# Two more tiles' first layer half by seven products, odd values copied by transfers, and one sum of each weight kept in place

## The chip, the cores and the metric

The kernel runs on one core of one Trainium2 chip. The metric is the device time of one execution in microseconds (us); it is the median of several runs. Engines are named as the profile names them: PE (matrix products), PEld (the loading of their stationary operand), DVE (vector), ACT (scalar functions), POOL, and SP, which here only issues transfers. A small q behind a name is that engine's sequencer.

## The reference

Sliding-window attention over 8 batches of 8 heads with 576 positions of 64 values each, followed by two matrix products with a gated function between them. All rows of the attention output go through the two layers.

```python
scores = scale * np.matmul(q, k.transpose(0, 1, 3, 2))
mask = np.abs(pos[:, None] - pos[None, :]) <= 32
attn = softmax(np.where(mask, scores, -1e9))
x = np.matmul(attn, v)                     # -> 4608 rows of 512
h = x @ w_in                               # 512 x 2048
g = h * (1.0 / (1.0 + np.exp(-1.702 * h)))
out = g @ w_out                            # 2048 x 512
```

## The kernel before

The 4608 rows are 36 units of 128; two units make a tile `t` of 256 rows (18 tiles). The program first works through a head (tiles 0 to 2), then `window(4)`, then one `steady(w)` for each w from 5 to 18, and `close()`. In `steady(w)` PE makes the attention of units 2w and 2w+1, the first layer of tile w-1 and the second layer of tile w-2. Every engine executes its instructions in the order in which the program emits them.

A first layer can be made in two ways. `layer1(t, d)` is the plain one: eight products of 128x128 by 128x256 into one bank, then one ACT pass; eight such calls make a tile. The other way makes half of the tile's first layer (the columns 512 to 1023 and 1536 to 2047 of `w_in`) by the seven products of a fast 2x2 block multiplication, and the other half by four calls of `layer1`. `seven(t, n)` is one of these products: eight matrix instructions of 128x128 by 128x128. It needs sums of blocks of `w_in` (`wi_sum`, made once) and sums of blocks of the tile (`x_sums`, made by DVE). Partial results are moved out of the two banks `h_main` and `h_side` by `move`.

```python
def bank(self, kind, shape, dtype, name):        # PSUM: 8 banks in all, with the pair "a" below
    bufs = {"h": 2, "o": 1, "t": 1, "b": 2}[kind]
    return self.ps.tile(shape, dtype, name=name, tag=kind, bufs=bufs)

def pair(self, name, which=None):                # two banks: "a", or both buffers of "b"; in turn
    if which is None:
        which, self.turn = self.turn, 1 - self.turn
    if which == 0:
        return self.ps.tile([128, 2, 512], F32, name=name, tag="a", bufs=1)
    return [self.bank("b", [128, 512], F32, f"{name}{i}") for i in range(2)]

def odd_v(self, m, eng):                         # values shifted by 64 rows
    ...
    self.cast(eng, vo[64:128], self.ve[m % NV][64:128])
    self.cast(eng, vo[0:64], nxt)

def layer1(self, t, d, kind="h"):
    ...
    ffs = (d, d + 8) if t > 2 else (2 * d, 2 * d + 1)
    ...    # 2 x 4 products into one bank of the given kind, then ACT: g <- gelu(bank)

def norm(self, u):                               # DVE: x <- values / sum, frees the banks of values(u)
    ...

# head(), from the first layer of tile 2 on (cut)
    self.layer1(2, 0)
    self.values(6)
    self.norm(6)
    for n in range(2):
        self.w_sums(n, 1)
    for d in range(1, 3):
        self.layer1(2, d)
    self.x_T(6, "b")
    self.layer1(2, 3)
    for hp in range(4):
        self.rows_T("k", 2, hp, "t", dve)
        if hp in (1, 2):
            self.w_sums(hp + 1, 1)
        self.rows_T("q", 2, hp, "o", act)
        self.layer1(2, 4 + hp)
    for m in (7, 8, 9):
        self.odd_v(m, dve)

# window(4): its end (cut)
    self.loads(w)
    for m in (10, 11):
        self.odd_v(m, dve)
    self.w_in_sums((0, 1))
    for d in range(8):
        self.layer1(w - 1, d)
    self.g_sums(w - 1, 0)
    self.feed(w)
    self.w_in_sums((2, 3))

def steady(self, w):                             # cut to its order; t = w - 1, o = w - 2
    self.loads(w)
    self.scores(a, which=0); self.scores(b, which=1)
    self.g_sums(o, 1, (0, 1))
    self.product(o, 1, "o")
    self.keep(o, 1, dve)                         # reads the bank that product 6 adds to
    if w > 5:
        self.g_sums(o, 0, (2,))
    self.product(o, 2, "t")
    self.result(o, 11)
    ...
    self.product(o, 6)
    ...
    self.seven(t, 1); self.move("side", "main", dve); self.x_sums(t, (0, 1))
    self.values(a, which=0); self.values(b, which=1)
    self.norm(a); self.x_T(a)                    # x_T: a transposing transfer issued by SP
    ...
    self.norm(b); self.x_T(b)
    ...
    self.product(o, 4); self.result(o, 21, act)  # result 21 stores unit b of tile o (SP)
    ...
    self.feed(w)                                 # odd_v of units 2w+2, 2w+3; then rows_X (SP)
    ...
    self.product(o, 3); self.result(o, 12)       # stores unit a of tile o (SP)
```

`values(u)` of the next window reads what `odd_v(u)` made in this one. `rows_X` are four transposing transfers of later keys and queries.

Of the kernel before, what the change touches and what calls it, by code (L numbers as in the profile page):

```python
# [15 lines left out]
F32 = mybir.dt.float32  # L16
# [11 lines left out]
class _Kernel:  # L28
# [7 lines left out]
    def __init__(self, ctx, tc, q, k, v, w_in, w_out, out):  # L36
        self.tc, self.nc = tc, tc.nc
        self.q, self.k, self.v, self.w_in, self.w_out, self.out = q, k, v, w_in, w_out, out
        self.B, self.H, self.S, self.D = q.shape
        self.N = self.B * self.S  # L40
        self.DM = self.H * self.D
        self.DFF = w_in.shape[1]
        self.NK = self.DM // 128
        self.NFF = self.DFF // 128
        self.scale = 1.0 / (self.D ** 0.5)
        self.NU = self.N // 128
        self.NW = self.NU // 2

        def pool(name, bufs, **kw):
            return ctx.enter_context(tc.tile_pool(name=name, bufs=bufs, **kw))  # L50

        self.cst = pool("cst", 1)
        self.work = pool("work", 2)
        self.ps = pool("ps", 1, space=bass.MemoryType.PSUM)
        self.stage, self.paired = {}, set()
        self.span = {"A": (0, 320)}
        self.xT, self.g, self.o_ps = {}, {}, {}
        self.p, self.acc, self.x, self.sc = {}, {}, {}, {}
        self.gs, self.part, self.o_sb = {}, {}, {}
        self.xs, self.hs, self.turn = {}, {}, 0  # L60

    def bank(self, kind, shape, dtype, name):
# [15 lines left out]
    def setup(self):  # L78
# [3 lines left out]
        self.w_in_sb = cst.tile([128, self.NK, self.DFF], F16, name="w_in_sb")  # L82
        self.wi_sum = cst.tile([128, 4, 2, self.DFF // 4], F16, name="wi_sum")
        self.ident16 = cst.tile([128, 128], F16, name="ident16")
        self.w_out_sb = cst.tile([128, self.NFF, self.DM], F16, name="w_out_sb")
        self.w_sum = cst.tile([128, 4, self.NFF // 2, self.DM // 2], F16, name="w_sum")
        self.kT = cst.tile([128, 4, RING + 64], BF16, name="kT")
# [88 lines left out]
    def odd_v(self, m, eng):  # L176

        vo = self.vo[m % NV]
        nxt = self.v_first if m == self.NU - 1 else self.ve[(m + 1) % NV][0:64]
        self.cast(eng, vo[64:128], self.ve[m % NV][64:128])  # L180
        self.cast(eng, vo[0:64], nxt)

# [180 lines left out]
    def layer1(self, t, d, kind="h"):  # L363
# [5 lines left out]
        else:  # L369
            hps = self.bank(kind, [128, 2, 256], F32, "h_ps")  # L370
        ffs = (d, d + 8) if t > 2 else (2 * d, 2 * d + 1)
        for i in range(2):
# [21 lines left out]
    def w_sums(self, i, half):  # L394

        b, w, dve = self.w_out_sb, self.w_sum, self.nc.vector
        top, low = slice(4 * half, 4 * half + 4), slice(8 + 4 * half, 12 + 4 * half)
        left, right = slice(0, 256), slice(256, 512)
        t = [w[:, n, top, :] for n in range(4)]
        a, c = [(b[:, top, right], b[:, top, left]), (b[:, low, right], t[0]),  # L400
                (b[:, low, right], b[:, top, right]), (b[:, low, left], t[1])][i]
        dve.tensor_sub(t[i], a, c)
# [19 lines left out]
    def product(self, t, n, kind=None):  # L422
# [10 lines left out]
        for k in range(8):  # L433
            x, y = {1: (g[:, k, u], b[:, k, left]), 2: (g[:, 8 + k, u], b[:, 8 + k, left]),
                    3: (gs[:, 3, k], b[:, 8 + k, right]), 4: (g[:, 8 + k, v], w[:, 3, k]),
                    5: (gs[:, 0, k], w[:, 0, k]), 6: (gs[:, 1, k], w[:, 1, k]), 7: (gs[:, 2, k], w[:, 2, k])}[n]
            nc.tensor.matmul(self.part[t, key], x, y, start=(first and k == 0), stop=(k == 7), skip_group_check=True)  # L437
# [45 lines left out]
    def head(self):  # L483
# [79 lines left out]
        dve.tensor_copy(self.q_first, self.qT[:, :, 0:32])  # L563
        for n in range(4):
            self.w_sums(n, 0)
# [12 lines left out]
        for hp in range(4):  # L578
            self.rows_T("k", 1, hp, "b", dve)
            self.rows_T("q", 1, hp, "b", act)  # L580
            run(1)
        self.scores(4)
        self.scores(5)
# [26 lines left out]
        for c in "kq":  # L610
            self.load_rows(c, 3, (0, 1))
        self.layer1(2, 0)
        self.values(6)
        self.norm(6)
        for n in range(2):
            self.w_sums(n, 1)
        for d in range(1, 3):
            self.layer1(2, d)
        self.x_T(6, "b")
        self.layer1(2, 3)  # L620
        for hp in range(4):
            self.rows_T("k", 2, hp, "t", dve)
            if hp in (1, 2):
                self.w_sums(hp + 1, 1)
            self.rows_T("q", 2, hp, "o", act)
            self.layer1(2, 4 + hp)
        for m in (7, 8, 9):
# [8 lines left out]
    def w_in_sums(self, which):  # L636
# [3 lines left out]
        for n in which:  # L640
            x, y = [(w[:, top, v], w[:, low, v]), (ws[:, 0], w[:, top, u]),
                    (w[:, top, u], w[:, top, v]), (w[:, low, u], ws[:, 1])][n]
            (self.nc.vector.tensor_sub if n else self.nc.vector.tensor_add)(ws[:, n], x, y)

# [10 lines left out]
    def seven(self, t, n):  # L655

        hs = self.hs
        if n == 1:
            self.xs[t] = self.work.tile([128, 4, 2, 128], F16, name="xs", tag="xs", bufs=1)
            self.g[t] = self.work.tile([128, self.NFF, 256], F16, name="g", tag="g", bufs=2)  # L660
            hs["main"], hs["side"] = (self.bank("h", [128, 4, 128], F32, name) for name in ("h_main", "h_side"))
# [3 lines left out]
        for f in range(4):  # L665
            here = slice(128 * f, 128 * f + 128)
            top, low = slice(512 + 128 * f, 640 + 128 * f), slice(1536 + 128 * f, 1664 + 128 * f)
            for k in range(2):
                a, b = {1: (w[:, k, top], x[:, k, u]), 2: (w[:, 2 + k, top], x[:, 2 + k, u]),
                        3: (ws[:, 3, k, here], x[:, 2 + k, v]), 4: (w[:, 2 + k, low], xs[:, 3, k]),  # L670
                        5: (ws[:, 0, k, here], xs[:, 0, k]), 6: (ws[:, 1, k, here], xs[:, 1, k]),
                        7: (ws[:, 2, k, here], xs[:, 2, k])}[n]
                self.nc.tensor.matmul(dst[:, f], a, b, start=(n in (1, 7) and f == 0 and k == 0),  # L673
                                      stop=(f == 3 and k == 1), skip_group_check=True)

    def move(self, key, src, eng, add=None):

        if key != "side":
            self.hs[key] = self.work.tile([128, 2, 4, 128], F32, name="hs", tag="kc" if key[0] == "k" else "qc")[:, 0]
        if add is None:  # L680
# [19 lines left out]
    def steady(self, w):  # L700
# [10 lines left out]
        self.keep(o, 1, dve)  # L711
        if w > 5:
            self.g_sums(o, 0, (2,))
        self.product(o, 2, "t")
# [26 lines left out]
        else:  # L741
            self.layer1(t, 0, "a")
        if w > 5:
            self.g_sums(o, 0, (3,))
        self.g_sums(o, 1, (3,))
# [23 lines left out]
        self.product(o, 3)  # L769
        self.result(o, 12)  # L770

    def window(self, w):
# [31 lines left out]
        for m in (10, 11):  # L804
            self.odd_v(m, dve)
        self.w_in_sums((0, 1))
        for d in range(8):
            self.layer1(w - 1, d)
        self.g_sums(w - 1, 0)
        self.feed(w)  # L810
        self.w_in_sums((2, 3))

# [24 lines left out]
    def feed(self, w):  # L837

        dve = self.nc.vector
        for m in (2 * w + 2, 2 * w + 3):  # L840
            if 11 < m < self.NU:
                self.odd_v(m, dve)
        i = (w + 3) // 2
# [63 lines left out]
```

## Time and profile before

| | |
|---|---|
| time, median of 3 runs (range) | 285.85 us (285.62 to 286.61) |
| span of the profiled execution | 284.3 us |
| granted PE clock | 1.00 |
| first layer, plain: x704 matrix instructions, mean 273 ns each | 83.4 us |
| copies of odd values by DVE: x71, mean 341 ns | 24.2 us |
| transposing transfers of `x` by SP: x28, issue to landing | 7.1 us (median) |
| stores of 256 KB by SP: x34, issue to landing | 4.9 us (median) |

The page of a profile gives busy time by engine, the span in 40 slices, and groups of instructions with their mean duration. A matrix instruction's duration is mostly latency: the instructions overlap, so what one costs is read from the distance of starts in the timeline of PE, not from its mean. Idle time of an engine that is not the bottleneck costs nothing.

### The profile page before, as it was taken

The page shows a single profiled execution, that of the slowest core. Times are in us where ns is not written, and L with a number is a line of the kernel's source. Part 1 is how long each engine was busy: PE and PEld are TensorE (multiplying, and loading weights), DVE is VectorE, ACT ScalarE, POOL GpSimd, SP SyncE. Part 2 cuts the span into 40 slices and gives each one's busy share as a digit, 9 for nine tenths or more (in the row PEclk, how much of TensorE's full clock was granted, in tenths as well). Part 3 has the DMA queues.
Part 4 walks back from the last instruction along what each step waited for, and adds up shares of the span by engine and source line. Part 5 has one row for each costly group of instructions (what it writes and reads, how often), then busy time and mean ns, then how long its engine had stood idle before and what let it go on. Part 6 is the DMA issues. An engine that isn't in the chain of part 4 may idle for free. (4 is left out here: it accounts for less than half of the span.)

```text
span 284.3 us, 9735 instructions
## 1 busy us (share of the span) xinstructions
PE 277.7 (98%) x4093; PEld 234.4 (82%) x4094; DVE 222.7 (78%) x600; ACT 194.8 (69%) x311; POOL 102.1 (36%) x140
## 2 busy tenths in 40 slices
PE   7989999999999999999999999999999999999994
PEld 2668665866899989999989888999999999999983
DVE  7851467678798979898979797979797979796663
ACT  4576457685778787878686867777777777776340
POOL 8955424998627333742525343422000000000000
PEclk9999999999999999999999999999999999999999
DMA  9999999999999999999999999999844321212022
GB/s 152 190 198 205 200 183 166 170 136 126 196 134 146 147 146 152 151 172 167 146 176 145 153 156 155 200 150 158 145 75 114 74 70 48 71 45 71 24 76 74
DMA packets 144827, 38.84 MB, mean 137 GB/s; under 512 B 129936, under 2 KB 140432, under 8 KB 144784
## 3 DMA queue, kind: packets, MB, share of 16 engines
q0 software_dynamic: 97232, 18.16, 84.5%
q1 hardware_dynamic: 47104, 19.67, 42.6%
q8 instruction: 32, 0.52, 0.8%
q10 hardware_dynamic: 448, 0.39, 0.5%
q14 instruction: 11, 0.09, 0.1%
HBM read 36.96 MB, written 9.44 MB: 163 GB/s over the span
## 5 line engine op out<-in xcount | busy, mean ns | idle before, releaser
L375 PE MATMUL h_ps<-xT,w_in_sb 128*128 128x256 f16 x704 | 83.4, 273 | 0.2
L375 PEld LDWEIGHTS <-w_in_sb 128*128 128x128 f16 x704 | 67.2, 98 | 8.1 <-DMA w_in_sb<-in_moe_w_in_dram 0.5
L377 ACT ACTIVATE g<-h_ps 128x512 f16<-128x512 f32 x88 | 52.2, 595 | 29.9 <-PE h_ps L375 27.9
L173 POOL DMA_DIRECT2D ve<-in_v_dram x41 | 34.4, 850 | 61.4 <-PE pv L326 43.6
L437 PEld LDWEIGHTS <-gs 128*128 128x128 f16 x480 | 45.2, 98 | 5.9 <-issue 0.3
L437 PE MATMUL o_ps<-w_sum,gs 128*128 128x256 f16 x360 | 44.3, 273 | 0.1
L437 PEld LDWEIGHTS <-g 128*128 128x128 f16 x360 | 34.1, 98 | 4.6 <-issue 0.3
L437 PE MATMUL o_ps<-w_out_sb,g 128*128 128x256 f16 x240 | 29.0, 273 | 0.0
L161 POOL DMA_DIRECT2D qs<-in_q_dram x27 | 22.8, 854 | 15.6 <-DMA ks<-in_k_dram 10.4
L673 PEld LDWEIGHTS <-wi_sum 128*128 128x128 f16 x448 | 27.4, 98 | 0.3
L119 DVE COPY vo<-ve 64x528 bf16<-64x528 bf16 x71 | 24.2, 341 | 4.2 <-DMA ve<-in_v_dram 2.3
L161 POOL DMA_DIRECT2D ks<-in_k_dram x27 | 22.9, 863 | 4.0 <-DMA ve<-in_v_dram 3.4
L307 DVE TENSOR_TENSOR p<-p,mask 128x1024 bf16<-128x1024 bf16 x32 | 21.9, 686 | 2.3 <-ACT p L297 2.1
L387 PE MATMUL o_ps<-w_out_sb,g 128*128 128x512 f16 x96 | 23.2, 380 | 0.0
L119 DVE COPY part<-o_ps 128x256 f32<-128x256 f32 x45 | 18.8, 418 | 5.4 <-PE o_ps L437 5.4
L688 ACT ACTIVATE g<-h_side 128x512 f16<-128x512 f32 x14 | 8.4, 597 | 21.5 <-DVE x L337 20.2
L673 PEld LDWEIGHTS <-w_in_sb 128*128 128x128 f16 x336 | 22.3, 98 | 1.0
L455 DVE TENSOR_TENSOR o_sb<-o_ps,part 128x256 f32<-128x256 f32 x45 | 19.0, 421 | 2.7 <-PE o_ps L437 0.8
L295 ACT ACTIVATE p<-sc 128x512 bf16<-128x512 f32 x36 | 19.5, 598 | 1.9 <-PE sc L287 1.9
L474 ACT ACT_TABLE_LOAD x15 | 19.2, 1283 | 0.3
L297 ACT ACT_TABLE_LOAD x15 | 19.2, 1283 | 0.3
L297 ACT ACTIVATE p<-sc 128x1024 bf16<-128x1024 f32 x18 | 18.4, 1024 | 1.3 <-PE sc L287 1.2
(104 smaller groups left out, 446.8 us busy)
## 6 DMA issues: line engine op xcount, KB each, us to landing
out_dram<-o_sb SPq DMA_DIRECT2D x34, 256.0 KB, 4.9
ve<-in_v_dram POOLq DMA_DIRECT2D x31, 128.0 KB, 9.0
ks<-in_k_dram POOLq DMA_DIRECT2D x24, 128.0 KB, 12.2
qs<-in_q_dram POOLq DMA_DIRECT2D x24, 128.0 KB, 12.4
w_in_sb<-in_moe_w_in_dram POOLq DMA_DIRECT2D x4, 512.0 KB, 9.5
w_out_sb<-in_moe_w_out_dram POOLq DMA_DIRECT2D x4, 512.0 KB, 14.0
ve<-in_v_dram POOLq DMA_DIRECT2D x10, 64.0 KB, 6.6
ks<-in_k_dram POOLq DMA_DIRECT2D x7, 64.0 KB, 11.1
```

Of the source, the lines that this page charges most:

```text
L119: (eng.copy if eng is self.nc.scalar else eng.tensor_copy)(out, in_)
L161: self.nc.gpsimd.dma_start(self.stage[key][off:off + m, n], src[b, :, s:s + m, :].rearrange("h s d -> s h d"))
L173: self.nc.gpsimd.dma_start(self.ve[m % NV][lo + off:lo + off + n, :, :self.D], self.v[b, :, s:s + n, :].rearrange("h s d -> s h d"))
L295: nc.scalar.activation(p[:, eo], sc[eo], AF.Exp, scale=self.scale)
L297: nc.scalar.activation(p.rearrange("k e h s -> k e (h s)"), both, AF.Exp, scale=self.scale)
L307: self.nc.vector.tensor_mul(pv, pv, msk.to_broadcast([128, 8, 2, SQ]))
L375: nc.tensor.matmul(hps[:, i, :], self.w_in_sb[:, kr, ff * 128:(ff + 1) * 128], self.xT[t][:, kr, :], start=(i == 0 and kr == 0), stop=(i = ...
L377: nc.scalar.activation(self.g[t][:, ffs[0]:ffs[1] + 1:ffs[1] - ffs[0], :], hps, AF.Gelu_apprx_sigmoid)
L387: nc.tensor.matmul(o_ps, self.g[t][:, ff, s * 128:(s + 1) * 128], self.w_out_sb[:, ff, :], start=(ff == 0), stop=(ff == self.NFF - 1))
L437: nc.tensor.matmul(self.part[t, key], x, y, start=(first and k == 0), stop=(k == 7), skip_group_check=True)
L474: self.nc.scalar.activation(self.spark, self.spark, AF.Gelu_apprx_sigmoid)
L673: self.nc.tensor.matmul(dst[:, f], a, b, start=(n in (1, 7) and f == 0 and k == 0), stop=(f == 3 and k == 1), skip_group_check=True)
```

## The change

It does three things. Tiles 2 and 3 (the third and the fourth) get half of their first layer by the seven products too, as the later tiles have it; for that the products are woven into the end of the head (tile 2), and `window(4)` gets a `chain` (tile 3). The odd values of units 10 and up are copied by transfers that SP issues, and no longer by DVE. And one of the four block sums of each weight is written over the block that is needed no more, which frees a quarter of `wi_sum` and of `w_sum`.

```diff
-        for n in range(4):
+        self.w_in_sums((0, 1, 3))
+        for n in (0, 1, 3):
             self.w_sums(n, 0)
@@ head, after the rows of keys and queries of block 1
+        self.w_in_sums((2,))
         self.scores(4)
@@ head, first layer of tile 2
-        self.layer1(2, 0)
+        self.room = self.work.tile([128, 4, 4, 128], F32, name="hs", tag="gs")
+        self.layer1(2, 0, "b")
         self.values(6)
+        self.seven(2, 1)
+        self.move("side", "main", dve)
         self.norm(6)
-        ... (w_sums, layer1(2, 1..7), rows_T; shown above)
+        self.x_sums(2, (0, 1))
+        self.layer1(2, 1, "b")
+        rows(0)                      # rows_T of k ("t", dve) and of q ("o", act)
+        self.x_sums(2, (2, 3))
+        self.seven(2, 2)
+        self.gelu(2, "side", 0, 0)
+        self.seven(2, 6)
+        self.move("k2", "main", act)
         self.x_T(6, "b")
+        self.layer1(2, 2, "b")
+        rows(1)
+        self.w_sums(0, 1)
+        self.seven(2, 7)
+        self.move("k7", "side", act)
+        self.seven(2, 5)
+        self.move("22", "main", dve, "k7")
+        rows(2)
+        self.layer1(2, 3, "b")
+        self.gelu(2, "22", 1, 1)
+        rows(3)
+        self.w_sums(1, 1)
+        self.seven(2, 4)
+        self.move("21", "side", dve, "k2")
+        self.seven(2, 3)
+        self.gelu(2, "main", 0, 1)
+        self.gelu(2, "21", 1, 0)
+        self.room = None
+        self.w_sums(3, 1)
@@ the block sums: number 2 of w_in, and of w_out, in place
-            (self.nc.vector.tensor_sub if n else self.nc.vector.tensor_add)(ws[:, n], x, y)
+            dst = (ws[:, 0], ws[:, 1], w[:, top, v], ws[:, 2])[n]
+            (self.nc.vector.tensor_sub if n else self.nc.vector.tensor_add)(dst, x, y)
-        t = [w[:, n, top, :] for n in range(4)]
+        t = [w[:, 0, top, :], w[:, 1, top, :], b[:, top, right], w[:, 2, top, :]]
@@ steady: both conditions fall away
-        if w > 5:
-            self.g_sums(o, 0, (2,))
+        self.g_sums(o, 0, (2,))
@@ window(4)
         for m in (10, 11):
-            self.odd_v(m, dve)
-        self.w_in_sums((0, 1))
-        for d in range(8):
-            self.layer1(w - 1, d)
-        self.g_sums(w - 1, 0)
-        self.feed(w)
-        self.w_in_sums((2, 3))
+            self.odd_v(m, self.nc.sync)
+        self.chain(w - 1, ("a", "b", "b", "a"), lambda: self.feed(w))
+        for half in range(2):
+            self.w_sums(2, half)
+        self.g_sums(w - 1, 0, (0, 1))
@@ feed
             if 11 < m < self.NU:
-                self.odd_v(m, dve)
+                self.odd_v(m, self.nc.sync)
@@ chain(t, kinds, between): new, without attention between its parts (cut)
+        self.seven(t, 1); self.move("side", "main", dve); self.x_sums(t, range(4))
+        self.layer1(t, 0, kinds[0]); self.layer1(t, 1, kinds[1])
+        self.seven(t, 2); self.gelu(t, "side", 0, 0)
+        self.seven(t, 6); self.move("k2", "main", act)
+        self.layer1(t, 2, kinds[2])
+        self.seven(t, 7); self.move("k7", "side", act)
+        self.seven(t, 5); self.move("22", "main", dve, "k7")
+        between()
+        self.layer1(t, 3, kinds[3]); self.gelu(t, "22", 1, 1)
+        self.seven(t, 4); self.move("21", "side", dve, "k2")
+        self.seven(t, 3); self.gelu(t, "main", 0, 1); self.gelu(t, "21", 1, 0)
```

## The prediction, made before the result was known

> **What bounds the kernel now.** I read the page first: busy times, then the slices.
>
> ```profile
> PE 277.7 (98%) x4093; PEld 234.4 (82%) x4094; DVE 222.7 (78%) x600; ACT 194.8 (69%) x311; POOL 102.1 (36%) x140
> DMA  9999999999999999999999999999844321212022
> ```
>
> PE is never idle, but its busy time is modelled, so this does not yet say that PE never waits. The second line says that transfers are dense until slice 28 of 40, about 200 us. Then I asked for the busy time of each engine by stretch: the first layer of tile 2, that of tile 3, two steady windows. The columns are microseconds busy with the instruction count, in the order PE, PEld, DVE, ACT, POOL, then clock, DMA share, GB/s.
>
> ```profile
> 50.20:59.77 9.57, 9.57 (x117) 8.42 (x115) 6.97 (x14) 6.67 (x12) 9.57 (x14) 1.00 1.52 157
> 69.25:76.33 7.08, 7.08 (x65) 6.15 (x63) 5.72 (x15) 4.76 (x8) 4.37 (x5) 1.00 1.77 165
> 133.19:147.40 14.21, 14.21 (x226) 12.85 (x225) 12.20 (x34) 10.73 (x18) 5.25 (x6) 1.00 1.80 167
> 218.66:232.87 14.21, 14.21 (x227) 12.84 (x226) 12.20 (x34) 10.73 (x18) 0.00 (x0) 1.00 0.32 77
> ```
>
> A window takes 14.21 us with heavy transfers and with few, so it is PE's own work and nothing else. The timeline of PE (start, duration; the distance of starts is the cost) gives that work's prices:
>
> ```profile
> 50.20 1.04 PE L375 MATMUL h_ps<-xT,w_in_sb 128*128 128x256 f16 x8
> ...
> 51.55 1.92 PE L375 MATMUL h_ps<-xT,w_in_sb 128*128 128x256 f16 x16
> ...
> 76.97 1.92 PE L437 MATMUL o_ps<-w_out_sb,g 128*128 128x256 f16 x16
> 78.72 1.91 PE L437 MATMUL o_ps<-w_sum,gs 128*128 128x256 f16 x16
> ...
> 82.53 0.61 PE L673 MATMUL h_side<-xT,w_in_sb 128*128 128x128 f16 x8
> 82.98 0.61 PE L673 MATMUL h_main<-xs,wi_sum 128*128 128x128 f16 x8
> 83.43 1.05 PE L375 MATMUL h_ps<-xT,w_in_sb 128*128 128x256 f16 x8
> 84.32 1.04 PE L437 MATMUL o_ps<-w_sum,g 128*128 128x256 f16 x8
> ```
>
> A seventh product costs 0.45 us (82.53 to 82.98), a plain call 0.87 us (64 instructions in the 7.08 us of tile 3: 0.11 each). So DVE's relief is worth nothing in the windows by itself, and every new wait of PE is paid in full, since PE never has spare time later to catch up.
>
> **What the skill says.** The Trainium skill, "TensorE: Matmul & The Clock Gate", section "Back-to-back issue gap", gives N/2.4 + 2.5 ns for a warm product: 55.8 ns at 128 columns, 109.2 at 256. The trace agrees (0.45/8 = 56, 0.11); the sustained 81 ns at 128 columns, which it names for streams with weight loads, is not seen here. "PSUM — Partial Sum Buffer", section "Engine vs sequencer instructions": queues of DVE and ACT are strict FIFO and products start in program order. The trace's order agrees; so one blocked instruction holds all behind it. "DMA: Bandwidth & Descriptors", section "Queues, rings and completion order": each DMA engine takes an issuer's descriptors in ring order and goes round robin between issuers. That fits SP's stores here: 7.6 us to landing in the median from 84 to 206 us, 2.2 from 210 to 260, when the loads are over.
>
> **The change, part by part.**
>
> *Products.* Per tile four plain calls (4 x 0.873 = 3.49 us) become seven of 0.447 (3.13): -0.36, for two tiles -0.72 us. This is the whole of what can be won.
>
> *Tile 2's weave.* I laid the new order over the trace's durations. `layer1(2, 0)` now takes a buffer of "b", of which there are two, and `values(6)` wants both (its two-part `norm` in the trace shows that it uses "b").
>
> ```profile
> 51.34 0.60 ACT L377 ACTIVATE g<-h_ps 128x512 f16<-128x512 f32 x1 [0.35 <-PE h_ps L375]
> ```
>
> That pass frees the buffer at 51.94, but the second half of `values(6)` could start at 51.36: PE waits until 52.00, 0.64 us. Next, DVE's order is `move`, then `norm(6)`, and `layer1(2, 1, "b")` needs a bank that `norm(6)` frees. `seven(2, 1)` starts at 52.19; in the windows the copy starts 0.86 later (80.47 to 81.33), so 53.05, next DVE start 0.60 on: 53.65; reciprocal 0.21, multiply 0.42: 54.28. PE resumes at 54.34, having been done at 52.74: 1.60 us lost. From there, with 0.22 per transpose group, a gelu starting 1.08 after its plain call and a move 0.65 after its product, I get `rows(3)` at 60.31, but its bank "t" is freed by the copy of `rows(2)`, which stands in DVE behind move "22", which waits for ACT's "k7" (done 59.43): 60.1 + 0.7, so 0.54 us more. The attention of unit 7 starts at 62.26 instead of 59.77. There ACT's last gelu waits for move "21", which DVE makes behind a row copy and a weight sum (62.5 to 63.1); gelu to 63.9, table load 1.28, exponential 1.02: 66.18, and `scores(9)`, which wants that bank, would be ready at 65.58: 0.66 us. Sum of waits 3.44.
>
> *Window 4 and 5.* In the chain two plain calls stand between copy and use, and I find no wait of PE. But DVE now has, behind "21", two sums `w_sums(2)` (0.60 each), and four `g_sums` (0.79 a pair), before `keep` of product 1, and product 6 adds to the bank that `keep` reads. Before:
>
> ```profile
> 78.05 0.42 DVE L119 COPY part<-o_ps 128x256 f32<-128x256 f32 x1
> ```
>
> and product 6 followed at 78.72. On the clock of before, the chain ends 0.36 early, at 75.97; "21" ends at 76.3, then 1.2 + 1.58: `keep` at 79.1 to 79.5, product 6 at 79.55 where PE could have had it at 78.35: 1.2 us.
>
> *Block sums.* In place or not, the count stays the same, and those moved to the head fall into DVE's idle 5.4 us before 27.25: nothing.
>
> *Transfers of odd values.* About 1.4 us of DVE per window goes, worth nothing. In exchange four transfers of 64 x 1056 bytes stand in SP's queue between the store of result 21 and the rows:
>
> ```profile
> 140.10 3.44 SPq L355 DMA_TRANSPOSE xT<-x  x2
> 143.63 0.78 SPq L466 DMA_DIRECT2D out_dram<-o_sb  x1
> 144.50 2.73 SPq L168 DMA_TRANSPOSE kT<-ks  x2
> 147.33 3.78 SPq L168 DMA_TRANSPOSE qT<-qs  x2
> ```
>
> This store landed 7.3 us after issue, at 150.96; `values` of the next window begins at 152.07. One fourth of a store's bytes each, so by my estimate some 0.25 to 0.5 us each behind it (stores and xT landed 0.6 to 2.3 apart): the last of four at 152.0 to 153.0, needed at 152.4. Over windows 6 to 13 the same margin is 0.2 to 1.1 us, so a few of them wait: some 1.2 us in all, from 0 to 5. Later nothing. SP itself has 2 to 2.6 us idle per window, and four issues take about 2.
>
> Sum: -0.72 + 3.44 + 1.2 + 1.2 = +5.1, less a little because later moves of the weave may overlap better than by my table: 290.6 us.
>
> **Rivals.** *The gain comes through* (285.2 us): if the banks were free in time. For it: the same weave runs without a wait in the windows. Against it: there, plain calls stand between the move and its users, here `values` takes the banks. *SP's queue becomes the bound*: the transposes already take 8 us to land, and a late odd value stops PE in eight windows; at 0.8 us each it is 6 us more, 296. For it: DMA is full there and the margin is under a transfer's length; against it: small transfers, and every wait of PE gives the loads more time. *The relief of DVE pays*: would need PE to wait for DVE in windows; they are 14.21 all along, only one has 14.43; at most 0.2 us.
>
> **Range and chances.** The head's 2.2 us are hardly avoidable, the other waits are each uncertain by half; odd values add only upward. 287.3 to 294.3 holds it 8 times in 10. Two per cent is 291.6. Faster by over 2%: 0.02; within: 0.60; slower: 0.38.
>
> **What would show it.** Per step: starts of seventh products in the head 0.45 apart; a hole in PE of about 0.6 us inside `values(6)` and of 1.6 us before the next plain call, put down to ACT g and DVE x; the first scores of window 4 near 62.3; a wait before product 6 of window 5 on DVE's `part`; in windows 6 to 13 a PE wait on a transfer into vo, windows longer than 14.21 there and equal to it later. I am wrong if the head shows no holes (then about 285), or if windows to 13 grow by over 0.6 each (then over 294).

## The result and the profile after

The changed kernel takes 295.67 us (median of 4, 294.84 to 296.38) where the kernel before takes 285.97 us (285.62 to 286.61): a ratio of 1.0336, interval 1.0302 to 1.0369. It is slower by 9.7 us. The prediction said 290.6, with 294.3 as the upper end.

The page of the changed kernel, its busy times:

```profile
PE 280.6 (95%) x4142; PEld 236.4 (80%) x4142; DVE 212.4 (72%) x562; ACT 196.3 (67%) x315; POOL 102.2 (35%) x140
```

DVE lost 10.3 us of work, as the change intends. PE's share fell from 98% to 95% in a span of 294.1 us: PE waits now.

Where it waits is seen by stretch. The columns are those of the table before; the stretches run from the first scores of one window to those of the next, and are in turn the weave of tile 2 with the attention ahead of it, window 4 (tile 3), and windows 5, 6, 7 and one after the loads have ended.

```profile
42.57:63.85 21.28, 19.06 (x286) 13.62 (x285) 14.91 (x33) 14.22 (x24) 15.95 (x22) 1.00 1.31 153
63.85:80.94 17.09, 16.32 (x246) 11.31 (x244) 12.82 (x32) 12.11 (x19) 13.47 (x16) 1.00 2.41 151
80.94:96.36 15.42, 14.37 (x226) 12.83 (x224) 12.64 (x33) 11.71 (x20) 5.26 (x6) 1.00 2.27 158
96.36:111.78 15.42, 14.61 (x225) 13.03 (x225) 11.13 (x30) 10.73 (x18) 6.25 (x8) 1.00 1.98 174
111.78:126.69 14.91, 14.61 (x225) 13.02 (x225) 11.13 (x30) 10.73 (x18) 5.75 (x7) 1.00 1.99 163
214.33:228.54 14.21, 14.21 (x226) 12.84 (x226) 11.03 (x30) 10.73 (x18) 0.00 (x0) 1.00 0.58 120
```

Before, these stretches took 18.91, 16.56, 14.23 and then 14.21 us. In every line where the first number is above PE's busy time, PE stood still for about the difference. The sum of all differences, in us:

```
start of the scores of unit 4 (40.87 -> 42.57)          +1.70
weave of tile 2                (18.91 -> 21.28)          +2.37
window 4                       (16.56 -> 17.10)          +0.54
window 5                       (14.23 -> 15.42)          +1.19
windows 6 to 13   +1.21 +.70 +.30 0 +1.26 -.22 +.84 0 =  +4.08
last window                                              -0.07
span                           (284.3 -> 294.1)          +9.8
```

The first line need not be the change's. Up to there PE runs the same program in every kernel of this case (in the changed head DVE has more block sums to make), and the scores of unit 4 start at 40.87, 41.02 and 42.24 in three kernels with the head of before, and between 40.71 and 42.57 in nine with that of after. These are single executions, and the two ranges lie over each other.

The waits of PE, from its timeline (start, duration, in brackets the idle time ahead and what ended it). First the head and window 4:

```profile
53.69 0.19 PE L330 MATMUL pv<-ve,p 128*64 128x65 bf16 x1 [0.50 <-ACT g L381]
55.96 1.05 PE L379 MATMUL h_ps<-xT,w_in_sb 128*128 128x256 f16 x8 [1.40 <-DVE x L348]
...
57.29 0.61 PE L705 MATMUL h_side<-xT,w_in_sb 128*128 128x128 f16 x8
57.73 0.61 PE L705 MATMUL h_main<-xs,wi_sum 128*128 128x128 f16 x8
...
62.42 0.38 PE L196 MATMUL tp<-ident,kc 128*128 128x128 bf16 x4 [0.32 <-DVE kT L120]
67.78 0.45 PE L291 MATMUL sc<-qT,kT 64*64 64x128 bf16 x24 [0.54 <-ACT p L301]
```

The four foreseen holes stand in the foreseen places, behind the foreseen releasers: `values(6)` behind ACT's g, `layer1(2, 1)` behind the norm, `rows(3)` behind the copy of keys, `scores(9)` behind the exponential. The seventh products themselves are 0.45 us apart (57.29, 57.73). Then product 6 of window 5, after product 1 at 81.58:

```profile
84.55 1.91 PE L441 MATMUL o_ps<-w_sum,gs 128*128 128x256 f16 x16 [1.05 <-DVE part L120]
```

It waits on `part`, the copy of `keep`.

Window 4 holds a loss and a saving. The first line below is its attention and second layer before, the other two are the same stretch after, and the first layer of tile 3 behind it:

```profile
59.77:69.25 9.48, 9.48 (x157) 4.97 (x157) 7.37 (x20) 6.87 (x9) 9.17 (x11) 1.00 2.27 131
63.85:74.23 10.38, 9.61 (x158) 5.07 (x157) 10.05 (x23) 7.50 (x10) 7.92 (x10) 1.00 2.10 162
74.23:80.94 6.71, 6.71 (x89) 6.24 (x87) 2.77 (x9) 4.61 (x9) 5.55 (x7) 1.00 2.88 134
```

The plain first layer of tile 3 took 7.08 us (69.25 to 76.33), so the chain saves 0.37 there, all that was hoped for. The stretch ahead of it loses 0.90: `scores(9)` starts 3.93 us into the window where it was 3.33, and `values(7)` loses 0.30 more in a wait for DVE's `p`.

And in the windows from 6 on:

```profile
101.80 0.22 PE L330 MATMUL pv<-vo,p 128*64 128x65 bf16 x1 [0.54 <-DMA vo<-ve]
102.51 0.22 PE L330 MATMUL pv<-vo,p 128*64 128x65 bf16 x1 [0.26 <-DMA vo<-ve]
117.42 0.22 PE L330 MATMUL pv<-vo,p 128*64 128x65 bf16 x1 [0.28 <-DMA vo<-ve]
161.01 0.22 PE L330 MATMUL pv<-vo,p 128*64 128x65 bf16 x1 [0.72 <-DMA vo<-ve]
190.85 0.22 PE L330 MATMUL pv<-vo,p 128*64 128x65 bf16 x1 [0.62 <-DMA vo<-ve]
```

The table of waits has these five waits of products, 2.4 us in all, and seven of the weight loads of the same line, which stand ahead of the products, 3.4 us in all; so a window loses more than the bracket of its product shows.

What SP does about one of these windows (start, duration of the issuing, how many):

```profile
121.29 1.19 SPq L359 DMA_TRANSPOSE xT<-x  x1
122.57 0.53 SPq L470 DMA_DIRECT2D out_dram<-o_sb  x1
123.16 2.56 SPq L183 DMA_DIRECT2D vo<-ve  x4
125.81 2.57 SPq L169 DMA_TRANSPOSE kT<-ks  x2
```

The four transfers sit between store and rows as drawn, and take 2.56 us to issue. On the page they need 6.4 us from issue to landing:

```profile
vo<-ve SPq DMA_DIRECT2D x51, 66.0 KB, 6.4
```

### The profile page after: what moved, and what is told of

It reads as the page before. It is cut to its first block, busy times and chain, and to the rows that moved or that the text cites. A ratio compares the mean times of both kernels' runs of the same rounds, so it can differ in the third digit from the quotient of the medians.

```text
span 294.1 us, 9896 instructions
## 1 busy us (share of the span) xinstructions
PE 280.6 (95%) x4142; PEld 236.4 (80%) x4142; DVE 212.4 (72%) x562; ACT 196.3 (67%) x315; POOL 102.2 (35%) x140
## 5 line engine op out<-in xcount | busy, mean ns | idle before, releaser
L379 PE MATMUL h_ps<-xT,w_in_sb 128*128 128x256 f16 x640 | 76.3, 273 | 1.7 <-DVE x L348 1.4
L381 ACT ACTIVATE g<-h_ps 128x512 f16<-128x512 f32 x80 | 47.4, 595 | 31.6 <-PE h_ps L379 29.5
L379 PEld LDWEIGHTS <-w_in_sb 128*128 128x128 f16 x640 | 60.9, 98 | 8.8 <-DVE x L348 1.6
L705 PEld LDWEIGHTS <-w_in_sb 128*128 128x128 f16 x512 | 33.8, 98 | 1.6
L718 DVE TENSOR_TENSOR hs<-h_side,hs 128x512 f32<-128x512 f32 x16 | 11.1, 691 | 29.4 <-PE h_side L705 29.4
L441 PE MATMUL o_ps<-w_out_sb,gs 128*128 128x256 f16 x240 | 31.1, 273 | 0.1
L441 PE MATMUL o_ps<-w_sum,gs 128*128 128x256 f16 x240 | 28.6, 272 | 1.0 <-DVE part L120 1.0
L723 ACT ACTIVATE g<-h_side 128x512 f16<-128x512 f32 x16 | 9.6, 598 | 26.2 <-DVE x L341 11.9
L705 PEld LDWEIGHTS <-wi_sum 128*128 128x128 f16 x384 | 23.5, 98 | 0.0
L723 ACT ACTIVATE g<-hs 128x512 f16<-128x512 f32 x32 | 19.9, 623 | 1.0 <-DVE hs L718 1.0
L330 PEld LDWEIGHTS <-p 128*64 128x64 bf16 x576 | 12.0, 110 | 9.5 <-DMA vo<-ve 3.4
```

What stands on the lines that cost most here:

```text
L379: nc.tensor.matmul(hps[:, i, :], self.w_in_sb[:, kr, ff * 128:(ff + 1) * 128], self.xT[t][:, kr, :], start=(i == 0 and kr == 0), stop=(i = ...
L381: nc.scalar.activation(self.g[t][:, ffs[0]:ffs[1] + 1:ffs[1] - ffs[0], :], hps, AF.Gelu_apprx_sigmoid)
L723: self.nc.scalar.activation(self.g[t][:, at:at + 4, 128 * v:128 * v + 128], self.hs[src], AF.Gelu_apprx_sigmoid)
```

## Experiments

Theory: two independent costs. About 4 us lie in the head and window 5, in waits for banks and for DVE's order; the rest in windows 6 to 13 is odd values that land too late, and only because they are late. Rivals: the transfers cost as such, because SP or the DMA engines are full; the waits of the head are nested, so that mending one of them only uncovers the next.

### Odd values of units 12 and up by DVE again

```diff
-                self.odd_v(m, self.nc.sync)      # feed
+                self.odd_v(m, dve)
```

> The changed kernel, but DVE copies the odd values of units 12 and up again, in the windows where it did before; only units 10 and 11 stay with transfers. Theory (PE waits for late odd values, 4.1 to 4.3 us in windows 6 to 13 of the trace): those windows fall back to 14.21 us, total 295.7 - 4.2 = 291.5, 291.0 to 292.0. Rival (the lengthening of those windows is general transfer load or a new order of sums, and the odd values are only where it shows): less than 2 us come back. For the 1.7 us that the trace shows before 21 us, where the program is unchanged: if it comes with the new memory layout it stays in this run's trace, first scores near 8.8 us; if it is chance they are near 7.8.

Measured 290.37 us, ratio 1.0134 (1.0097 to 1.0171). By stretch (weave, windows 4, 5, 6):

```profile
40.93:62.21 21.28, 19.07 (x286) 13.62 (x285) 14.92 (x33) 14.23 (x24) 15.92 (x22) 1.00 1.52 162
62.21:79.36 17.15, 16.32 (x246) 11.31 (x244) 12.88 (x32) 12.12 (x19) 13.54 (x16) 1.00 2.50 150
79.36:94.77 15.41, 14.37 (x226) 12.83 (x224) 13.80 (x37) 11.71 (x20) 5.26 (x6) 1.00 2.12 158
94.77:108.98 14.21, 14.21 (x225) 12.84 (x224) 12.55 (x34) 10.73 (x18) 6.25 (x8) 1.00 1.96 163
```

All windows from 6 on are 14.21 again, while weave, window 4 and window 5 are as in the changed kernel. So the two costs are separate. The transfers of odd values from unit 12 on cost 1.0336 - 1.0134 = 2.0%, about 5.8 us; all the rest of the change costs 1.34%, about 3.8 us. The two intervals together (the root of their squares) leave about 1.4 us to either side of the 5.8. The profiled execution of the changed kernel holds 4.1 us of it in the windows 6 to 13; where the rest lies is not shown.

### The transfers alone, in the kernel before

```diff
-                self.odd_v(m, dve)               # feed, and window(4) likewise
+                self.odd_v(m, self.nc.sync)
```

> The kernel before with one part of the change alone: odd values of units 10 and up copied by SP's transfers, at the places of the change. Theory: +4.2 us from waits of PE for vo in windows 6 to 13, total 290.0, 289 to 291.5. Rival (transfers do harm only because the changed head shifts the windows against the loads): under +2 us. First scores near 7.8 us if the early loss belongs to the new layout, since the layout here is that of before.

Measured 294.05 us, ratio 1.0256 (1.0226 to 1.0286): +7.3 us, more than expected. Six of the windows 6 to 13 are longer than 14.21; window 6 takes 18.27. Its wait, from PE's timeline:

```profile
98.22 0.22 PE L329 MATMUL pv<-vo,p 128*64 128x65 bf16 x1 [2.19 <-DMA vo<-ve]
```

A hole of 2.19 us doesn't explain 4.06. The microseconds after it do; the number behind the engines is the granted clock of PE:

```profile
99.00:100.00 1.00, 1.00 (x11) 0.91 (x10) 0.25 (x1) 0.00 (x0) 1.00 (x2) 0.72 1.78 154
100.00:101.00 1.00, 1.00 (x12) 1.00 (x10) 0.96 (x5) 0.39 (x1) 1.00 (x2) 0.50 1.60 158
101.00:102.00 1.00, 1.00 (x8) 0.80 (x7) 0.93 (x5) 0.69 (x2) 0.75 (x2) 0.50 2.17 157
102.00:103.00 1.00, 1.00 (x8) 0.69 (x6) 0.80 (x3) 0.10 (x1) 0.43 (x2) 0.58 1.61 158
103.00:104.00 1.00, 1.00 (x14) 0.92 (x12) 0.00 (x0) 0.64 (x2) 0.57 (x1) 1.00 1.38 299
```

After the hole the clock is at half for some 3.4 us, and the window needs 16.08 us of PE for work that takes 14.20. So one late odd value costs twice: the wait, and then about 1.9 us of a slow PE. The Trainium skill, "TensorE: Matmul & The Clock Gate", section "Part 1: The HAM clock gate (the "warmup" mystery)", has the half clock and its 3.4 us, but lets it come after an idle window of about 3.4 us; here 2.19 us of waiting were enough. The section on ACT's transfers below shows what decided it.

### Tile 2's weave: another bank, and the norm before the move

```diff
-        self.layer1(2, 0, "b")
+        self.layer1(2, 0, "o")
         self.values(6)
         self.seven(2, 1)
-        self.move("side", "main", dve)
         self.norm(6)
+        self.move("side", "main", dve)
```

> The changed kernel with two edits in tile 2's weave: its first plain call takes bank o instead of one of the two b, and norm(6) stands ahead of the move in DVE's order. Theory: both holes of PE (0.50 and 1.40 us by the trace, 0.64 and 1.60 by starts) go, total 295.7 - 2.2 = 293.5, 293.1 to 293.9. Rival (the later waits of the weave, on the row copy and on the exponential, take over): 1 us or less comes back.

Measured 295.51 us, ratio 1.0304 (1.0251 to 1.0356), which the transfers' chance hides: in this run one window had 17.78 us. But the weave went from 21.28 to 19.65, and in its timeline both holes are gone, for one new small one (the wait of 0.32 us behind the copy of keys stays):

```profile
50.80 1.05 PE L379 MATMUL h_ps<-xT,w_in_sb 128*128 128x256 f16 x8 [0.22 <-DVE o_sb L120]
```

So these two waits are the bank of `values(6)` and the order of move and norm: -1.63, where the holes were 0.69 and 1.57 by starts of products. The 17.78 us window has the same pattern as the one above: a hole of 1.62 us on vo and a clock of 0.90 over the window.

The same edit with the odd values by DVE, so that the windows are still:

> The weave's two edits (bank o for the first plain call, norm(6) ahead of the move) again, but on the kernel in which DVE copies the odd values of units 12 and up, so that the chance in the transfers' landing doesn't cover them. That base was 1.0134 times before (+3.8 us). Theory (the two holes cost what they show): the stretch from the scores of unit 4 to those of unit 7 falls from 21.28 to 19.65 us, as it did in the trace of the earlier run, and the time by 1.6 to 2.2 us: 1.0070 times before. Rival (later waits take the gain): 1.011 or more.

Measured 289.11 us, ratio 1.0113 (1.0070 to 1.0157), against 1.0134 without the edit; the intervals overlap. The weave is 19.97 (-1.31), but window 4 rises from 17.15 to 17.68. In the run before, with the same edit, window 4 took 16.80. The difference is a wait at `values(7)`. The first two lines are from this run, and the third is from the run before, which has no such wait:

```profile
67.53 0.22 PE L330 MATMUL pv<-ve,p 128*64 128x65 bf16 x1 [0.81 <-DVE p L311]
62.86 4.01 DVE L120 COPY vo<-ve 64x528 bf16<-64x528 bf16 x6
62.22 2.85 DVE L120 COPY vo<-ve 64x528 bf16<-64x528 bf16 x6
```

Ahead of `p`, DVE makes the six copies of odd values of units 7 to 9 that end the head. They start 1.49 us into the window in both runs, and take 4.01 us in one and 2.85 in the other; in the kernels of this case the same six take 2.0 to 4.5 us, single ones 0.29 to 0.87. Why they vary is not shown. So the half microsecond is the price of slow copies in this execution, and not given back because of the edit. What the edit is worth in time stays open: the medians differ by less than their intervals.

### Sums of w_out earlier in window 4

```diff
         self.x_sums(t, range(4))                 # chain
+        for half in range(2): self.w_sums(2, half)
...
-        for half in range(2): self.w_sums(2, half)   # behind the chain
         self.g_sums(w - 1, 0, (0, 1))
```

> On the same base: the two block sums w_sums(2) that stand behind the chain are made in it, right after the sums of x, where DVE is idle for some 2.7 us. Theory (product 6 of window 5 waits for keep, and that for these sums): window 5 from 15.41 to 14.23 us, time 1.2 us less, 1.009 times before. Rival (the four sums of g alone already hold keep back): window 5 stays above 14.8.

Measured 290.27 us, ratio 1.0137 (1.0109 to 1.0165): no gain in time. In the trace product 6 follows product 1 (79.73) without a wait, and a later wait takes its place:

```profile
81.49 1.91 PE L441 MATMUL o_ps<-w_sum,gs 128*128 128x256 f16 x16
84.53 0.22 PE L330 MATMUL pv<-ve,p 128*64 128x65 bf16 x1 [0.30 <-DVE p L311]
```

In the trace window 5 falls from 15.41 to 14.87, so the cause of the wait is right and its removal brings 0.54 of 1.2. The rival's number (above 14.8) came true, but not its reason. What holds `p` now is ACT, whose table load for the exponential stands behind the last gelu of the chain: it starts 1.36 us after the window's first scores, where it was 0.73 before.

### The transfers 5.6 us earlier

```diff
+            for m in (2 * w + 2, 2 * w + 3):     # top of steady, behind loads(w)
+                if m < self.NU:
+                    self.odd_v(m, self.nc.sync)
...
-                self.odd_v(m, self.nc.sync)      # feed
```

> The changed kernel with the same transfers of odd values, issued at the top of the window before, ahead of the transposes of x, instead of behind its stores; same count, same bytes, same queue. Theory (only their lateness costs): windows 6 to 13 back at 14.21, total 291.5, 291.0 to 292.3. Rival (SP's queue or the DMA engines are full, so four more transfers per window cost whatever their place): PE then waits for xT or still for vo, total above 294.

Measured 291.61 us, ratio 1.0172 (1.0132 to 1.0212). All windows from 6 on are 14.21, but one of 14.35; `values` no longer waits on vo, though issue to landing takes 6.6 us. So neither the number of transfers nor their time was the cost, but that they were started too late: in windows 5 to 13 the first of a window is issued 11.0 to 12.6 us after the first scores in the changed kernel (median 11.4), and 5.3 to 7.1 us after them here (median 5.8).

The same in the kernel before:

> The kernel before, with the odd values of units 12 and up copied by transfers that SP issues at the top of the window before, and units 10 and 11 in window 4. Theory (lateness is what costs, not the transfers themselves): all windows from 6 on at 14.21, no wait on vo, time within 0.5 us of before. Rival (the four transfers per window also push the others, xT above all, back in SP's order): some windows 0.3 to 2 us longer with a wait on xT, +1.5 to +3 us in all, as the mended version with early transfers showed against that with DVE copies (2.8 us).

Measured 288.71 us, ratio 1.0049 (1.0023 to 1.0074), which is 1.4 us more than before. Single executions take 286.1 to 290.0 us; two more, of 291.3 and 291.8, are left out of the ratio. It is between theory and rival. In the profiled run the windows from 6 on are at 14.21 but for one, longer by 1.2, and window 5 (units 10 and 11, whose transfers stand in window 4) is longer by 1.0. Window 5 has this wait:

```profile
83.93 0.22 PE L329 MATMUL pv<-vo,p 128*64 128x65 bf16 x1 [0.80 <-DMA vo<-ve]
```

That is lateness again. The later window has a wait of 0.99 us at 199.06, for which the profile names no releaser; its odd values had landed by 195.01. It stays open.

### All mends together

Both versions have the bank and order edits (`values(6)` also stands ahead of `layer1(2, 0)`, and `rows(2)` ahead of move "22") and all sums of w_out's second half in the chain. One has the odd values from unit 12 on by DVE, the other by early transfers.

> All mends on the same base: values(6) ahead of the first plain call, that call in bank o, norm(6) ahead of the move, the copy of rows(2) ahead of move 22, all of the second half's w_sums inside the chain, and odd values of units 12 and up by DVE. Theory: every wait of the head goes but part of that for the exponential (0.2 to 0.5 us), and the 0.72 us of saved products show: 285.5 against 286.0 of before, 0.997 to 1.000 times. Rival (the seven products in the head are slower by more than their waits): above 1.003.

> The same mends, but the odd values by transfers issued early, at the top of the window before. Theory (an early transfer costs nothing): the same time as the version with DVE, within 0.3 per cent. Rival (DVE's relief is worth something once the head doesn't wait): faster than it by 0.3 us or more; or (transfers load the queue that brings xT) slower by 0.5 us or more.

With DVE copies: 286.78 us, ratio 1.0015 (0.9995 to 1.0034), no difference to before that can be measured. With early transfers: 290.19 us, ratio 1.0113 (1.0075 to 1.0152). By stretch, the first (weave, windows 4 and 5):

```profile
42.49:61.31 18.82, 18.71 (x285) 13.44 (x284) 14.78 (x32) 13.87 (x24) 13.51 (x19) 1.00 1.27 154
61.31:78.12 16.81, 16.62 (x248) 11.43 (x246) 13.71 (x35) 12.46 (x20) 13.54 (x17) 1.00 2.07 146
78.12:92.87 14.75, 14.55 (x227) 12.92 (x225) 13.00 (x35) 11.60 (x20) 6.74 (x8) 1.00 2.09 156
```

and the weave of the second:

```profile
41.74:60.28 18.54, 18.54 (x285) 13.52 (x284) 14.32 (x32) 13.86 (x24) 13.19 (x19) 1.00 1.29 160
```

18.54 is 0.37 below the 18.91 of before: the whole saving of seven products against four calls, once no hole is left. The first weave has it too. From the last transpose of `x` ahead of tile 2's products to the next window both versions take 10.30 us, where it was 10.66; the first loses 0.27 ahead of that transpose. In window 4 the chain takes 6.89 us for 7.08, but the stretch ahead of it takes 9.92 for 9.48: ACT's exponential starts 1.40 us after the first scores, 0.73 before, which is what is left of the fourth hole. So the mends don't win the time back: window 4 stays 0.2 above before, window 5 0.5. The second version also shows what early transfers can do elsewhere:

```profile
171.49 0.61 PE L702 MATMUL h_main<-xs,wi_sum 128*128 128x128 f16 x8 [1.34 <-DVE xs L681]
...
198.40 0.62 PE L702 MATMUL h_main<-xT,w_in_sb 128*128 128x128 f16 x8 [0.42 <-DMA xT<-x]
```

The product waits for xT itself, or for sums made from it. SP's own order says a part of why. In window 9 of each kernel, SP's first transpose of x is issued so long after the window's first scores (in windows 6 to 13, the two early versions have 8.4 to 9.6 and 9.1 to 11.1):

```
before            6.91 us      changed             6.91 us
early, unmended   8.69 us      early, all mends   11.13 us
```

With the four issues ahead of it (about 0.65 us each, 2.6 in all) SP runs late, and xT has no margin. Why SP is later still with all mends is not shown. So the rival of the full queue holds for the early version with all mends, but not for the changed kernel itself.

### The transfers issued by ACT

```diff
-                self.odd_v(m, self.nc.sync)      # feed
+                self.odd_v(m, self.nc.scalar)
```

> The changed kernel, but the odd values of units 12 and up are copied by transfers that ACT issues, at the same place of the program, so that they no longer stand behind SP's store and transposes. Backlog theory (the transfers are late because they stand behind the store and the transposes in SP's order): issue to landing falls from 6.4 us to under 4, the waits on vo in windows 6 to 13 fall from 4.3 us to under 1, and the time is that of the changed kernel with DVE copies, 290.4, plus up to 1 for ACT's issues: about 291. Jump theory (transfers in flight are held up by 1.7 to 2 us after a fetch of instructions, whoever issued them): jumps still appear between the landings of one window, but from an earlier start, so a part of the waits stays: about 292.5. Queue-length rival (SP has too many transfers to issue): also near 291, and transposes of x land earlier than in the changed kernel.

Measured 347.99 us, ratio 1.2174 (1.2134 to 1.2214). None of the expectations saw this. ACT's timeline in one window:

```profile
113.09 6.22 ACTq L183 DMA_DIRECT2D vo<-ve  x4
119.36 0.60 ACT L381 ACTIVATE g<-h_ps 128x512 f16<-128x512 f32 x1 [5.68 <-DMA vo<-ve]
```

ACT's sequencer is 6.22 us in the issuing of four transfers, and the gelu behind them stands still for 5.68 us. Three are issued at once (113.09, 113.71, 114.30 us), the fourth at 118.84. That is 0.07 us after the landing of SP's second transpose of x (118.77), and in all ten windows that have a fourth issue it comes 0.07 or 0.08 us after the same landing (98.65 to 98.72 and 139.29 to 139.36 in the windows beside it). So ACT's fourth issue waits for a transfer of SP; which wait of the program ties the two is not shown. The profile puts such stops of ACT, 58.1 us in eleven, down to the transfers; the kernel is slower by 61.6 us, and the mean clock of PE falls to 0.924. The run therefore says little of what it was made for. The landings came 4.6 us after issue in the median, where 6.4 were needed behind SP's store and transposes. The Trainium skill, "DMA: Bandwidth & Descriptors", section "Queues, rings and completion order", lets another issuer's transfers take turns with SP's; so the 1.8 us between the two may be the order in SP's ring, but with less dense transfers in this run (122 GB/s against 144) that isn't shown.

Its clock records show what the half clock hangs on. Every change of clock in this run lies on a grid of 3.41 us: the stretches at half clock last 3.41 or 6.83 us, those between them 13.65, 17.07 or 40.96. The first follows the weave's hole of 1.40 us. The number behind the engines is the clock; the first line is the step with the hole, the second the step after it:

```profile
51.60:55.02 3.42, 1.52 (x29) 1.17 (x24) 1.75 (x6) 0.57 (x1) 3.42 (x5) 1.00 1.15 198
55.02:58.43 3.41, 3.41 (x31) 3.19 (x30) 1.55 (x5) 1.78 (x3) 3.41 (x6) 0.50 2.08 132
```

The changed kernel has the same hole and keeps its clock. Laid over each trace from its own first change of clock on, the grid tells the cases apart by PE's idle time within one step:

```
kernel                 hole of PE                idle in its step   clock in the next step
transfers alone        96.03 to 98.22, 2.19      2.19               half
ACT's transfers        53.10 to 54.50, 1.40 *    1.90               half
weave, first edit      202.62 to 204.25, 1.62    1.62               half
weave, first edit      129.05 to 130.62, 1.57    0.75 and 0.82      full
changed                54.55 to 55.96, 1.40 *    0.96 and 0.94      full
* with the hole of 0.50 us ahead of it
```

In the last two the grid cuts the hole in two. In all kernels of this case, up to their last two steps, each step at full clock with 1.9 us or more of idle PE was followed by half the clock, and none with up to 1.5 us; at 1.62 us one was and one was not. So a hole's cost depends on where it falls on the grid, which differs from one execution to the next.

### Tile 2 alone

The kernel before, with tile 2's mended weave, tile 3 plain, four places for each weight's sums, DVE copies, and the sums of w_out's second half in window 4.

> The kernel before, with tile 2 alone by seven products, in the mended order (first call in bank o, norm before the move, rows before move 22), block sums of w_in in the idle head, all four kept in own places, sums of w_out's second half in window 4, tile 3 plain, odd values by DVE. Theory: the weave takes 18.5 to 18.8 us in place of 18.91, window 4 and 5 stay at 16.56 and 14.23, so 0.1 to 0.4 us less from the scores of unit 4 on, 285.8 where the kernel before has 286.1. Rival (waits are nested, and the next window pays what the weave gains): window 4 over 16.8, the time equal or above.

Measured 286.73 us, ratio 1.0015 (1.0004 to 1.0027). By stretch (weave, window 4):

```profile
42.27:61.01 18.74, 18.71 (x287) 13.45 (x286) 13.76 (x31) 13.87 (x24) 13.42 (x19) 1.00 1.26 155
61.01:78.00 16.99, 16.81 (x223) 11.30 (x222) 12.99 (x35) 12.41 (x19) 14.39 (x17) 1.00 1.99 149
```

The rival is right: the weave gains 0.17 and window 4 gives back 0.43. Here too the products themselves give 0.36 (10.30 us for 10.66 from the last transpose of `x` on), and 0.19 is lost ahead of them. In window 4 the plain first layer of tile 3 takes 7.08 us as before, and the stretch ahead of it 9.91 for 9.48, the same as in the version with all mends (9.92):

```profile
61.01:70.92 9.91, 9.73 (x159) 5.14 (x158) 7.58 (x21) 7.64 (x11) 9.91 (x12) 1.00 2.04 132
```

ACT is behind it again: its exponential starts 1.39 us after the first scores. No version here beats the kernel before.

### Why the landings are late

The prediction spaced the landings of a window's four transfers by 0.25 to 0.5 us, and so had the last 1 to 2 us behind the store ahead of them. In the eight windows of the changed kernel it is 1.3 to 3.9 us. From the traces of the six kernels in which SP issues these transfers in every window, I took the 150 gaps between one landing and the next of the same window, for transfers issued up to 206 us, and asked whether the fetch of a page of the core's own instructions ended in that gap (a packet of 16 KB on a queue of its own, 32 in an execution, one in about 8 us at this time, each 0.9 to 2 us long):

```
                      gap over 1.4 us   below   median gap
a fetch ends in it          17             3      1.78 us
none does                    1           129      0.43 us
```

So the ordinary gap was estimated right; what was missed is a jump of 1.5 to 2.2 us, and 17 of 18 jumps hold the end of an instruction fetch. With one fetch in 8 us, chance would put one into about every fourth gap of 1.8 us (an estimate from these two numbers). In the changed kernel, for example, a fetch from 114.7 to 115.9 us, landings at 114.86 and 116.65; a fetch from 188.7 to 189.8, landings at 189.10 and 190.81. The packets of the data themselves had ended by then, at 114.76 and 188.30. In eleven windows a fetch ended between the last data packet and the last landing; the landing came 2.1 to 2.6 us after the packet in ten of them, 0.8 in one. In the 36 others it came after 0.4 to 1.2 us, and once after 1.8. So in a jump the values are copied, and the signal of the landing is late. That the fetch causes it is argued from this coincidence; no run removes a fetch.

Not all of the lateness is a jump. Of the 4.1 us that windows 6 to 13 of the changed kernel grow by, 1.8 are in windows 7, 8 and 12, whose transfers have one. Windows 6 and 10 lose 2.5 us without: no gap between their landings is over 0.92 us. There the store ahead of the transfers landed 4.84 and 4.40 us into the window, where `values` wants its first odd value at 4.68; before, the same store landed at 4.10 and 3.56.

## Why the prediction was wrong

**Products, -0.72.** Right: 0.45 us each in the head; 0.36 for tile 2 where no hole is left (10.30 against 10.66), and 0.37 for tile 3 in the changed kernel itself (6.71 against 7.08). In no version did both reach the end of the kernel, because waits beside them took more.

**Tile 2's weave, 3.44 of waits.** Right in place and size. By starts of products the 0.64 is 0.69 and the 1.60 is 1.57 (2.02 from `seven(2, 1)` to the plain call, less 0.45); the 0.54 at `rows(3)` is 0.32 by its bracket, and the 0.66 at `scores(9)` is 0.60, which is also what the prediction's own 66.18 less 65.58 gives. Weave and window 4 together are longer by 2.91, where the prediction has 3.44 - 0.72 = 2.72; 0.30 of the 2.91 is the wait behind DVE's copies, which it did not have. It foresaw the attention of unit 7 at 62.26; without the 1.70 of the early head it is at 62.15.

**Window 5, 1.2.** Measured 1.19, on `part`. What the prediction did not have is that such a wait can't simply be taken away: with the sums moved, 0.5 of the 1.2 came back, since PE then meets the next wait, for ACT's exponential.

**Block sums, nothing; DVE's relief, nothing.** With DVE 1.2 us lighter in each window (12.20 to 11.03), no window was shorter than 14.2, so the second is right. Block sums in place have no run of their own; all mends with DVE copies, one sum in place, and tile 2 alone, all four in their own places, both take 1.0015 times before.

**Odd values, "some 1.2 us in all, from 0 to 5".** This is the step that failed. All else in the sum is +3.9; the kernel with DVE copies has +3.8. The transfers cost 5.8 us in the changed kernel by the times (4.1 in the windows of the profiled execution) and 7.3 in the kernel before, not 1.2. The mechanism is as told (the last of four lands after `values` wants it, only while the loads last), the size is not. The term that was too small is "0.25 to 0.5 us each behind it", which is 1 to 2 us from the store to the last landing: it measured 1.3 to 3.9. It leaves out the jumps of about 1.8 us, and it took the store's own landing as fixed, where 0.7 to 0.8 us more used up the margin of 0.2 to 1.1 in two windows. Nor did it know that a late odd value can halve PE's clock for 3.4 us: 1.9 of the 7.3 us.

**The rivals.** "SP's queue becomes the bound", 296, is near in number only: SP issued xT at 6.91 us into the window as before, and with as many transfers, issued earlier, the waits on vo were gone. "The gain comes through" fell with the head's four holes.

**The range.** By the prediction's own words it is wrong "if windows to 13 grow by over 0.6 each (then over 294)". They grew by 0.5 on the average in the profiled run; that, the head, window 5 and the 1.70 us ahead of unit 4's scores, whose cause is not shown, make up its time. The other three executions, 294.84 to 296.38, are above the range too. The transfers' part, from 0 to 5, should have had its middle well above 1.2, as there was no slack to lose.

## What to carry to other kernels

Before a copy leaves an idle engine for a transfer, compare the margin with the longest gap between landings in the trace, and with the spread of the landing ahead of them, not with the usual ones: a margin of 0.2 to 1.1 us was less than a jump of 1.8, and two stores that landed 0.7 to 0.8 later used it up. Issuing the same transfers 5.6 us earlier removed those waits. Where PE has no slack, a saving of 0.36 us in a stage is only worth doing if DVE and ACT have that slack in the same stage and the next: it came through in its own stage, and the next one lost it again behind ACT (0.43 us in window 4). And before a wait in one trace is put down to an edit, look at the same stretch in another run with that edit.

## What the runs showed of the hardware

- Landings of back-to-back transfers from one issuer jump by 1.5 to 2.2 us about when the core fetches a 16 KB page of instructions (17 of 18 jumps), while their data packets had ended 2.1 to 2.6 us before the last landing.
- PE's clock changes on a grid of 3.41 us. A step with 1.9 us or more of idle PE was always followed by half the clock, one with up to 1.5 us never; a hole of 1.57 us that the grid cut in two cost no clock, and one of 1.40 us with 0.50 us beside it in the same step did.
- A transfer issued by ACT held ACT's own work for up to 8.1 us: in ten of ten windows its fourth issue came within 0.08 us of a landing of SP's transpose.
- The same DVE copy of 64x528 values took 0.29 to 0.87 us, and six of them 2.0 to 4.5 us, from one execution to the next.
